# Attention weights of the first 16 head pairs: who divides by the sums, and how the small constant is added

## The chip, the cores and the metric

The kernel runs on one core of one Trainium2 chip. The metric is device time of one execution in microseconds (us), median of several runs. The engines are named as the profile names them: PE is TensorE's matmul, PEld its weight load, DVE is VectorE, ACT is ScalarE, POOL is GpSimd, SP is SyncE, which here issues DMAs. Line numbers such as L387 are lines of the kernel before.

## The reference

Three stages follow one another: attention in a window of 128 tokens with a bias that falls with distance, then an expert layer with a maximum of three products, then one with a gate.

```
scores = scale * q @ k.T ;  scores = where(mask, scores + bias, -1e9)      # 4 batches, 8 heads, 576 tokens, 64 wide
attn = exp(scores - max) ;  attn = attn / (sum(attn) + 1e-09) ;  x = attn @ v
h = max(max(x @ w1, x @ w2), x @ w3) ;  x = h @ w_out                      # 512 -> 768 -> 512, 2304 tokens
out = (silu(x @ w_gate) * (x @ w_val)) @ w_out2                            # 512 -> 1536 -> 512
```

## The kernel before

Attention is cut into units. A unit is 128 queries (or the last 64 of a batch) of one pair of heads; there are 80 units. The pairs are gone through in the order of `ORDER`, four pairs of heads for each entry. The first four entries of `ORDER` are called `NATIVE`; they are 16 pairs of heads and 24 units (8 + 4 + 8 + 4). Their scores are plain fp32 products, where the other 56 units use products of fp32r halves.

Each unit passes through four pieces, and pieces of following units are emitted between one another:

- `st_scores`: PE forms the scores of both heads; DVE picks the window (L358), adds the bias and takes the row minimum of the negated scores (L363); ACT takes the exponential and its row sums `sm`, one number for each of 128 rows and 2 heads (L368).
- `st_normalise`: 1e-9 is added to the 128x2 tile `sm` (on POOL at L376 for the native units, on DVE at L380 for the others), DVE takes the reciprocal `rc` (L382), and each head's 128x128 tile `z` is multiplied by its column of `rc`. Which engine does that is given by two letters, one for each head: `NORM0` for the first `K0` pairs (L385), `NORM` = "aa" (ACT for both, L391) for the others. "p" is POOL (L387), "v" is DVE (L389), "a" is ACT (L391).
- `st_transpose`: PE transposes both heads (L400), ACT copies the result out of PSUM (L412, or L408), and POOL masks it into two triangles (L416).
- `st_values`: PE multiplies by the values (L430 for native units), ACT rounds the result into the tile `x` (L436, L441), and POOL (or for the very first pairs DVE) forms the rest that rounding left (L107, the helper `low`).

The first expert layer is cut into six chunks of 384 tokens. A chunk's up products (18 groups of 12 matmuls, L156 to L158, all on the tile `x`) can begin when all four pairs of its tokens are through attention. The weights are prepared on the way: a raw pair of words goes through ACT (L118), three operations of DVE (L121, L122, L124), ACT again (L129) and DVE (L107). `spread` lays attention pieces, weight preparations and groups of matmuls between one another:

```
a0[0]()
spread(a0[1:], conv[:C0])                          # 12 native units, 2 weight tiles
spread(u[0], conv[C0:], a1[:cut1], early=EC)       # chunk 0, 7 weight tiles, 12 native units
spread(u[1][:SPLIT], conv_o, a1[cut1:] + a2[:cut2])
```

With the numbers set here `cut1` is all of `a1`, so all 24 native units lie in the first two of these stages. From this order and from planned durations and priorities a planner then fixes one instruction order for each engine, and each engine runs its own in that order: an instruction that waits holds up all that stands behind it on its engine. The chunks, the second layer and its token and weight preparation follow in the same manner; the second layer runs from about 460 us on.

Of the kernel before, what the change touches and what calls it, by code (L numbers as in the profile page):

```python
# [8 lines left out]
F32 = mybir.dt.float32  # L9
# [4 lines left out]
ALU = mybir.AluOpType  # L14
# [6 lines left out]
P = 128  # L21
# [36 lines left out]
N1, N2 = 21, 25  # L58
MB, TB, VB = 3, 1, 2
WARM, WN = 24, 256  # L60
NORM0, K0 = "pv", 16
AH = 0, 100
EC = 0
SPLIT = 12
# [7 lines left out]
def kernel(ctx: ExitStack, tc, *args):  # L72
    n = len(NATIVE)
    qs, ks, qks = (dict(zip(u, x)) for u, x in ((NATIVE, args), (NATIVE, args[n:]), (ORDER[n:], args[2 * n:])))
    vv, w123, wo1, wgv, wo2, out = args[-6:]
# [10 lines left out]
    nc = tc.nc  # L86
# [99 lines left out]
    def up_groups(c):  # L186

        n = CT
        m = {}

        def group(f, e):
            xt = x_t[c]
            ps = ps_m.tile([P, 512], F32, tag="m", name="ps1")
            for k in range(KD):
                mm3(ps[:, :n], w1[f, e], k * P, xt[k][:, 0, :n], xt[k][:, 1, :n], k == 0, k == KD - 1)
            with tc.high_priority(HIGH):
                if e == 0:
                    m[f] = tmp.tile([P, CT], F32, tag="m0", name="m0")
                    nc.scalar.copy(m[f][:, :n], ps[:, :n])
                else:  # L200
                    nc.vector.tensor_tensor(out=m[f][:, :n], in0=ps[:, :n], in1=m[f][:, :n], op=ALU.max)
                if e == 2:
                    ht = hp.tile([P, 2, n], F32R, tag="h", name="h")
                    pool_round(ht[:, 0, :], m[f][:, :n])
                    low(nc.gpsimd, ht[:, 1, :], m[f][:, :n], ht[:, 0, :])
                    hs[c, f] = ht

        return [lambda f=f, e=e: group(f, e) for f in range(NF1) for e in range(3)]
# [32 lines left out]
    small = ea("small", 2)  # L241
# [4 lines left out]
    bias = att.tile([P, H, P], BF16, name="bias")  # L246
    later = att.tile([P, 2, P], mybir.dt.int16, name="later")
    edge = att.tile([P, H, P], BF16, name="edge")


    first = {}
# [52 lines left out]
    def native(b, s):  # L304


        return (b, s) in NATIVE
# [64 lines left out]

    def st_normalise(u):
        m = u.mq
        if native(u.b, u.s):
            nc.gpsimd.tensor_scalar(  # L376
                out=u.sm[:m], in0=u.sm[:m], scalar1=1e-9, scalar2=1.0, op0=ALU.add, op1=ALU.mult
            )
        else:
            nc.vector.tensor_scalar(out=u.sm[:m], in0=u.sm[:m], scalar1=1e-9, scalar2=None, op0=ALU.add)  # L380
        rc = small.tile([P, 2], F32, tag="rc", name="rc")
        nc.vector.reciprocal(out=rc[:m], in_=u.sm[:m])  # L382
        for a in range(2):
            za, ra = u.z[:m, a], rc[:m, a:a + 1]
            how = (NORM0 if todo.index((u.b, u.s, u.p)) < K0 else NORM)[a]  # L385
            if how == "p":
                nc.gpsimd.tensor_scalar(out=za, in0=za, scalar1=ra, scalar2=1.0, op0=ALU.mult, op1=ALU.mult)  # L387
            elif how == "v":
                nc.vector.tensor_scalar(out=za, in0=za, scalar1=ra, scalar2=None, op0=ALU.mult)  # L389
            else:  # L390
                nc.scalar.activation(out=za, in_=za, func=AF.Copy, scale=ra)  # L391
# [125 lines left out]
    for t in range(len(units) + LV):  # L517
        if t >= LV:
            u = units[t - LV]
            steps.append(lambda u=u: soon(st_values, u))  # L520
            if t + 1 == len(units) + LV or (units[t + 1 - LV].b, units[t + 1 - LV].s) != (u.b, u.s):
                done_at.append(len(steps))
        if 0 <= t - LT < len(units):
            steps.append(lambda u=units[t - LT]: soon(st_transpose, u))
        if 0 <= t - LN < len(units):
            steps.append(lambda u=units[t - LN]: soon(st_normalise, u))
        if t < len(units):
            u = units[t]
            if u.j == SUBS[u.s][0]:
                i = todo.index((u.b, u.s, u.p))  # L530
                if i == 0:
                    steps.append(begin)
                steps.append(lambda u=u, i=i: (soon(st_scores, u), prep_next(i + 1), load_next(i + 2)))
            else:
                steps.append(lambda u=u: soon(st_scores, u))
# [246 lines left out]
        nc.tensor.matmul(ps[:, :WN], cold[:, :P], cold[:, :WN], start=True, stop=True)  # L782

    make_identity(nc, ident)
    tab, ones = zp.tile([P, 2, P], F32, tag="z", name="tab"), zp.tile([P, 2, P], F32, tag="z", name="ones")
    nc.gpsimd.iota(tab, pattern=[[0, 2], [1, P]], base=0, channel_multiplier=-1, allow_small_or_imprecise_dtypes=True)
    nc.vector.tensor_scalar(out=later, in0=tab, scalar1=0.0, scalar2=None, op0=ALU.is_gt)
# [16 lines left out]
    u = [up_groups(c) for c in SEQ]  # L804
# [142 lines left out]
```

## Time and profile before

| what | value |
|---|---|
| median of 3 runs | 856.21 us (856.02 to 856.42) |
| the profiled execution, its own time | 856.89 us |
| its span, first to last instruction | 855.2 us |
| PE busy | 836.0 us, 98% |
| DVE, ACT, POOL busy | 612.2, 422.9, 391.1 us |
| granted clock, mean | 0.996 of full speed |

Busy times are sums over one profiled execution. About 1.7 us of its time lie outside the span. A busy PE is not PE at its peak, since the ends of pipelined matmuls are modelled; the weight loads, one for each matmul, show better how densely it works.

### The profile page before, as it was taken

Reading aid. Unit: us, or ns where it says so; the run is one execution under the profiler, and the core shown is the slowest. Engines: PE = TensorE matmul, PEld = TensorE weight load, DVE = VectorE, ACT = ScalarE, POOL = GpSimd, SP = SyncE. Lnnn points to the kernel's source line nnn. Section 1 sums busy time; section 2 is a strip of 40 time slices with the busy share of each in tenths; the row PEclk is TensorE's granted clock in tenths of the full one; section 3 lists DMA queues with packets and bytes.
Section 4 is the critical chain, followed back from the end, with each engine's and each line's share of the span. In section 5 each row is a group of like instructions: output and inputs, shape, how many; then the busy total and the mean of one; then the engine's idle time right before and its main releaser. Section 6 shows DMA issues by size and latency. Waiting matters only on the chain.

```text
span 855.2 us, 14694 instructions
## 1 busy us (share of the span) xinstructions
PE 836.0 (98%) x4760; PEld 783.1 (92%) x4760; DVE 612.2 (72%) x1568; ACT 422.9 (49%) x1146; POOL 391.1 (46%) x575
## 2 busy tenths in 40 slices
PE   8898998999999999999999999999999999999998
PEld 6687897999999999999999999999999999999996
DVE  7999799778777787638978989995564854443342
ACT  6775676777667667525445555543422422212220
POOL 3688888469877667744323232221421211211110
PEclk9999999999999999999999999999999999999999
DMA  9664334333322232303367397733938422837322
GB/s 324 213 216 132 106 120 136 102 119 103 99 87 87 81 115 82 108 20 117 116 236 256 118 377 272 273 112 124 366 122 282 140 74 74 285 110 247 110 74 98
DMA packets 62780, 133.34 MB, mean 156 GB/s; under 512 B 6768, under 2 KB 24176, under 8 KB 61552
## 3 DMA queue, kind: packets, MB, share of 16 engines
q1 hardware_dynamic: 59248, 127.69, 44.2%
q10 hardware_dynamic: 3456, 4.72, 1.5%
q8 instruction: 37, 0.61, 0.3%
q14 instruction: 39, 0.32, 0.1%
HBM read 96.99 MB, written 35.39 MB: 155 GB/s over the span
## 4 chain that ended last, share of the span: by engine, by line
PE 79%; DVE 7%; POOL 5%; ACT 3%; issue 3%; DMA 2%; ACTq 0%; SPq 0%; POOLq 0%; DVEq 0%
PE ps L157 8%; PE ps L156 8%; PE ps L158 8%; PE pg L684 7%; PE pg L683 7%; PE pg L685 7%; PE po L765 6%; PE po L764 6%; PE po L763 6%; PE pc L684 3%; PE pc L683 3%; PE pc L685 3%; PE pv L447 2%; PE pt L400 1%; DVE wr L124 1%
## 5 line engine op out<-in xcount | busy, mean ns | idle before, releaser
L107 POOL TENSOR_TENSOR act<-h,act 128x384 fp32r<-128x384 f32 x72 | 79.9, 1130 | 287.3 <-ACT act L129 258.1
L157 PE MATMUL ps<-x,w 128*128 128x384 f32 x432 | 147.8, 342 | 0.7 <-POOL x L107 0.7
L158 PE MATMUL ps<-x,w 128*128 128x384 f32 x432 | 147.1, 341 | 0.0
L156 PE MATMUL ps<-x,w 128*128 128x384 f32 x432 | 146.4, 344 | 0.0
L683 PE MATMUL pg<-ya,u 128*128 128x384 f32 x360 | 120.6, 335 | 1.2 <-ACT s L706 1.2
L684 PE MATMUL pg<-ya,u 128*128 128x384 f32 x360 | 121.1, 336 | 0.0
L685 PE MATMUL pg<-ya,u 128*128 128x384 f32 x360 | 120.5, 335 | 0.0
L764 PE MATMUL po<-u,act 128*128 128x512 f32 x216 | 85.2, 395 | 0.0
L765 PE MATMUL po<-u,act 128*128 128x512 f32 x216 | 85.1, 396 | 0.0
L763 PE MATMUL po<-u,act 128*128 128x512 f32 x216 | 83.9, 389 | 0.0
L157 PEld LDWEIGHTS ps<-x,w 128*128 128x128 f32 x432 | 81.8, 189 | 1.9 <-POOL x L107 0.9
L416 POOL TENSOR_SCALAR_AFFINE_SELECT t<-pk 128x512 fp32r<-128x512 f32 (+2 forms) x128 | 74.0, 600 | 19.9 <-DVE pk L107 17.0
L156 PEld LDWEIGHTS ps<-x,w 128*128 128x128 f32 x432 | 81.4, 190 | 1.6 <-issue 1.0
L692 DVE TENSOR_TENSOR u<-pg,s 128x384 f32<-128x384 f32 x72 | 39.7, 553 | 59.8 <-PE pg L685 59.6
L158 PEld LDWEIGHTS ps<-x,w 128*128 128x128 f32 x432 | 81.7, 189 | 0.2 <-issue 0.2
L683 PEld LDWEIGHTS pg<-ya,u 128*128 128x128 f32 x360 | 67.6, 188 | 5.3 <-ACT s L706 1.5
L684 PEld LDWEIGHTS pg<-ya,u 128*128 128x128 f32 x360 | 67.6, 188 | 4.6
L368 ACT ACTIVATE z<-z,mn 128x128 f32<-128x128 f32 (+1 forms) x160 | 63.2, 398 | 10.8 <-DVE mn L363 9.6
L685 PEld LDWEIGHTS pg<-ya,u 128*128 128x128 f32 x360 | 67.6, 188 | 0.5
L720 ACT ACTIVATE h<-s 128x384 f32<-128x384 f32 x36 | 18.9, 524 | 91.1 <-DVE s L692 91.1
L118 ACT ACTIVATE wf<-wr 128x512 f32<-128x512 f32 (+2 forms) x57 | 40.0, 701 | 29.3 <-DVE wr L124 14.7
L692 DVE TENSOR_TENSOR u<-pc,u 128x384 f32<-128x384 f32 x72 | 39.9, 554 | 17.9 <-PE pc L685 17.5
(122 smaller groups left out, 2085.7 us busy)
## 6 DMA issues: line engine op xcount, KB each, us to landing
ya<-a_dram SPq DMA_DIRECT2D x56, 384.0 KB, 4.7
a_dram<-ya SPq DMA_DIRECT2D x42, 384.0 KB, 5.2
wr<-wgv SPq DMA_DIRECT2D x24, 512.0 KB, 4.6
wr<-w SPq DMA_DIRECT2D x9, 1024.0 KB, 5.2
qkr<-qk SPq DMA_DIRECT2D x32, 288.0 KB, 2.8
o_dram<-acc SPq DMA_DIRECT2D x36, 256.0 KB, 2.8
acc<-o_dram SPq DMA_DIRECT2D x36, 256.0 KB, 2.7
wr<-wo SPq DMA_DIRECT2D x12, 512.0 KB, 4.4
```

Source lines behind the costliest of these rows:

```text
L107: eng.tensor_tensor(out=out, in0=raw, in1=head.bitcast(F32), op=ALU.subtract)
L156: nc.tensor.matmul(ps, wh, xt_h, start=first, stop=False)
L157: nc.tensor.matmul(ps, wh, xt_l, start=False, stop=False)
L158: nc.tensor.matmul(ps, wl, xt_h, start=False, stop=last)
L416: nc.gpsimd.affine_select(out=t[:, i, :n, :, :m], in_=w[:, :n, :, :m], compare_op=op, fill=0.0, base=0, pattern=[[0, n], [0, 2], [-sign, m ...
L683: nc.tensor.matmul(o, wh, y[:, 0], start=first and k == 0, stop=False, skip_group_check=True)
L684: nc.tensor.matmul(o, wh, y[:, 1], start=False, stop=False, skip_group_check=True)
L685: nc.tensor.matmul(o, wl, y[:, 0], start=False, stop=k == 1, skip_group_check=True)
L692: nc.vector.tensor_tensor(out=o, in0=x, in1=y, op=ALU.add)
L763: nc.tensor.matmul(po, ah, w[:, 0], start=j == 0, stop=False)
L764: nc.tensor.matmul(po, ah, w[:, 1], start=False, stop=False)
L765: nc.tensor.matmul(po, al, w[:, 0], start=False, stop=j == PASS - 1)
```

## The change

`NORM0` goes from "pv" to "va": in the 24 native units the first head's tile is multiplied on DVE and the second on ACT, where it was POOL and DVE. And for all 80 units 1e-9 is added on DVE, as the sum of two tensors, with a new tile `eps` of 128x2 that one memset fills at the start; before, it was POOL's sum with a constant for the native units and DVE's sum with a constant for the others.

```diff
-NORM0, K0 = "pv", 16
+NORM0, K0 = "va", 16
...
+    eps = small.tile([P, 2], F32, tag="eps", name="eps", bufs=1)
...
     def st_normalise(u):
         m = u.mq
-        if native(u.b, u.s):
-            nc.gpsimd.tensor_scalar(
-                out=u.sm[:m], in0=u.sm[:m], scalar1=1e-9, scalar2=1.0, op0=ALU.add, op1=ALU.mult
-            )
-        else:
-            nc.vector.tensor_scalar(out=u.sm[:m], in0=u.sm[:m], scalar1=1e-9, scalar2=None, op0=ALU.add)
+        nc.vector.tensor_tensor(out=u.sm[:m], in0=u.sm[:m], in1=eps[:m], op=ALU.add)
         rc = small.tile([P, 2], F32, tag="rc", name="rc")
...
     make_identity(nc, ident)
+    nc.vector.memset(eps, 1e-9)
```

## Rows read from the trace of the kernel before

**Rows 1.** Stages: length, busy us (x) of PE, PEld, DVE, ACT, POOL; clock; DMA.

```profile
0.00:35.00 35.00, 28.92 (x172) 20.59 (x172) 29.56 (x126) 22.73 (x80) 18.00 (x43) 0.95 0.85 299
35.00:88.00 53.00, 48.68 (x299) 42.55 (x300) 46.58 (x112) 35.40 (x102) 43.45 (x63) 0.99 0.48 160
88.00:130.00 42.00, 40.99 (x253) 37.58 (x252) 37.44 (x115) 29.51 (x100) 35.34 (x53) 0.97 0.37 116
130.00:200.00 70.00, 67.11 (x421) 65.00 (x420) 58.28 (x200) 50.26 (x156) 47.11 (x87) 1.00 0.39 120
200.00:365.00 165.00, 165.00 (x1041) 161.37 (x1040) 120.75 (x439) 110.03 (x352) 121.88 (x217) 1.00 0.30 94
```

**Rows 2.** Chain that ended last, between 0 and 88 us: shares by line.

```profile
by line: issue 17.3%; POOL t L416 8.8%; POOL z L387 6.8%; ACT z L368 6.1%; PE sc L349 5.8%; DVE wr L124 5.5%; ACT wf L118 4.4%; POOL x L107 4.1%; ACT w L129 4.1%; POOL sm L376 3.8%; POOL r L107 3.5%; DMA qz<-q 3.2%; DVE sc L358 2.8%; DVE z 
```

**Rows 3.** Instruction groups, 0 to 88 us: xcount | busy us, mean ns | idle before, releaser.

```profile
L387 POOL TENSOR_SCALAR z<-z,rc 128x128 f32<-128x128 f32 x24 | 18.4, 765 | 7.5 <-DVE rc L382 6.0 <-PE sc L349 0.4 <-ACT x L436 0.4
L376 POOL TENSOR_SCALAR sm<-sm 128x2 f32<-128x2 f32 x24 | 6.8, 282 | 13.3 <-ACT z L368 10.5 <-ACT x L436 1.4
L389 DVE TENSOR_SCALAR z<-z,rc 128x128 f32<-128x128 f32 x24 | 8.0, 335 | 0.1
L382 DVE RECIPROCAL rc<-sm 128x2 f32<-128x2 f32 x24 | 3.8, 160 | 3.3 <-POOL sm L376 2.9
L121 DVE TENSOR_SCALAR wf<-wf 128x1024 int32<-128x1024 int32 x9 | 7.7, 859 | 0.2 <-ACT wf L118 0.2
L107 DVE TENSOR_TENSOR kl<-qkr,r 128x384 fp32r<-128x384 f32 x4 | 3.4, 862 | 0.0
```

**Rows 4.** Lines by themselves over the whole span: duration ns min/median/max.

```profile
L387 POOL TENSOR_SCALAR z<-z,rc x24: 366/424/1607, 9.6 to 82.9; 128x128 f32<-128x128 f32 x24
L376 POOL TENSOR_SCALAR sm<-sm x24: 191/192/1034, 6.7 to 80.1; 128x2 f32<-128x2 f32 x24
L389 DVE TENSOR_SCALAR z<-z,rc x24: 268/307/505, 9.5 to 80.9; 128x128 f32<-128x128 f32 x24
L391 ACT ACTIVATE z<-z,rc x112: 385/398/422, 97.3 to 361.4; 128x128 f32<-128x128 f32 x80, 64x128 f32<-64x128 f32 x32
L380 DVE TENSOR_SCALAR sm<-sm x56: 150/324/979, 95.9 to 360.2; 128x2 f32<-128x2 f32 x40, 64x2 f32<-64x2 f32 x16
L121 DVE TENSOR_SCALAR wf<-wf x57: 267/428/1498, 15.1 to 683.7; 128x512 int32<-128x512 int32 x36, 128x256 int32<-128x256 int32 x12, 128x1024 int32<-128x1024 int32 x9
L107 DVE TENSOR_TENSOR kl<-qkr,r x64: 406/562/1362, 67.7 to 336.2; 128x384 fp32r<-128x384 f32 x32, 128x256 fp32r<-128x256 f32 x32
L107 DVE TENSOR_TENSOR pk<-pt,pk x48: 275/409/426, 104.7 to 377.6; 128x256 f32<-128x256 f32 x32, 128x128 f32<-128x128 f32 x16
```

**Rows 5.** L380 alone by stretch: DVE busy (x), granted clock, DMA share.

```profile
88.00:200.00 112.00, 9.57 (x22) 0.99 0.38 119
```

**Rows 6.** Who waited for whom, 0 to 88 us: us in total, times, longest.

```profile
PEld pv L430 <- POOL t L416: 6.2, 8, 1.7
DVE rc L382 <- POOL sm L376: 2.9, 5, 1.0
```

**Rows 7.** Instructions of PE's weight loads in order of time, 83.7 to 90.5 us (x: how many merged).

```profile
83.74 0.19 PEld L158 LDWEIGHTS ps<-x,w 128*128 128x128 f32 x1
85.01 0.19 PEld L430 LDWEIGHTS pv<-t,rv 128*64 128x64 f32 x2 [1.08 <-POOL t L416]
86.35 0.42 PEld L430 LDWEIGHTS pv<-t,rv 128*64 128x64 f32 x6 [1.15 <-POOL t L416]
...
87.43 0.33 PEld L158 LDWEIGHTS ps<-x,w 128*128 128x128 f32 x1
...
89.99 0.33 PEld L157 LDWEIGHTS ps<-x,w 128*128 128x128 f32 x1
90.31 0.19 PEld L158 LDWEIGHTS ps<-x,w 128*128 128x128 f32 x1
```

**Rows 8.** The stage around them, columns as in rows 1.

```profile
80.00:90.00 10.00, 8.27 (x44) 7.39 (x42) 7.29 (x10) 4.39 (x11) 9.56 (x12) 0.84 0.18 58
```

## The prediction

> **What bounds the kernel now.** I read the busy times by stage first [rows 1]. From 200 to 365 us PE is busy in all of the time, and its weight loads in 161.4 of 165 us: there nothing but PE's own work sets the time. In the first 88 us this is not so. The loads are busy 20.6 of 35 us and 42.6 of 53 us, so against the dense stage (0.978 busy) about 13.6 + 9.3 = 23 us of loading time are missing; from 88 to 200 us it is 3.5 + 3.5 = 7 us more. What PE does later has to be done anyway, so a microsecond won or lost in the first 88 us, where all 24 native units lie, should arrive at the end nearly whole. That is where the change acts.
>
> The second view is the chain that ended last in these 88 us [rows 2]. It jumps from engine to engine: POOL's masks, POOL's multiplications (L387, 6.8% of 88 us = 6.0 us), POOL's sums (L376, 3.8% = 3.3 us), ACT's exponentials, DVE's weight preparation. So no engine alone bounds this stretch; it is the latency of the attention pieces, laid through queues that are nearly full. How full, is in rows 1: DVE 76.1 of 88 us, POOL 61.5, ACT 58.1. DVE is the fullest, and that is the danger for a change that gives it more to do.
>
> The third view is the spread of durations [rows 4]. POOL's multiplication takes 0.366 us at best, 0.765 us in the mean [rows 3] and 1.607 us at worst, and POOL's sum over two columns ranges from 0.191 to 1.034 us. ACT's same multiplication stays within 0.385 to 0.422 us. DVE's instructions of one tensor and a constant (L380, L121) stretch too, and so does a DVE sum of two tensors that both lie in SBUF (`kl`, up to 1.362 us), while one that reads PSUM (`pk`) stays at 0.275 to 0.426. DVE and POOL hold each other up; ACT is held up by neither.
>
> **Part 1: POOL's 48 instructions go.** POOL loses 18.4 + 6.8 = 25.2 us [rows 3] of its 61.5, or 41%. On the chain the two lines are 6.0 + 3.3 = 9.3 us. They are not all gained, since their successors stand in the same places. At their mean durations they are 6.0 / 0.765 = 8 multiplications and 3.3 / 0.282 = 12 sums. So −9.3 us, before what takes their place.
>
> **Part 2: ACT multiplies the second head.** 24 instructions of the shape of L391, 0.398 us each, 9.6 us more on an ACT that is busy 58.1 of 88 us: 77% after it. DVE keeps one head as before (24 of L389 at 0.335 us, now the first), so the later of the two heads is ACT's. Eight steps of the chain at 0.398 us: +3.2 us. Behind the waiting ACT instruction stand exponentials and PSUM copies of other units; that is a cost only where ACT waits for `rc`, and I leave it to the rivals.
>
> **Part 3: DVE adds 1e-9 as a sum of two tensors, for the native units.** No row shows two tensors of two columns. From below: DVE's reciprocal of the same size, 0.160 us, and the best L380, 0.150. From above: L380 between 88 and 200 us, 9.57 / 22 = 0.435 us, where POOL is busy 82.5 of 112 us, 74% [rows 1, 5]. After the change POOL would be busy about 36.3 of 88 us, 41%, so of the excess of 0.285 us I take 41/74: 0.150 + 0.158 = 0.31 us. Twelve on the chain: +3.7 us. The other twelve lie in DVE's queue and cost it 3.7 us as well. Against this, DVE is stretched less when 41% of POOL's work is gone: L389 is 24 x (0.335 − 0.268) = 1.6 us over its best, and the weight preparation and `kl` together some 5 us over theirs by the same reckoning (L121 alone 9 x (0.859 − 0.68) = 1.6, where 0.68 is my estimate from its smaller shape and the best L389; `kl` 4 x (0.862 − 0.55) = 1.25, estimated the same way). 41% of 6.6 us is 2.7 us. Net +1.0 us for DVE's queue.
>
> The Trainium skill, page "SBUF — State Buffer", section "Who interferes with whom", says that a DVE instruction with two SBUF inputs contends with a GpSimd instruction that reads SBUF, just as one in a two-port mode does. By that the sum of two tensors is no escape from POOL's lock; the `kl` rows above agree. Were it an escape, all 24 would cost 0.16 us and the sum would be 3.6 us better; the rows don't support that.
>
> **Part 4: the same sum in the other 56 units.** DVE did it before and does it after. From 88 to 200 us it is 22 x 0.285 = 6.3 us over its best [rows 5], from which the new form may recover nothing (it stretches like `kl`) or much. PE has only 1.0 + 2.9 us idle there [rows 1], so the gain is 0 to 3.9 us. I take −0.5 us: the `kl` instructions stretch nearly as far. From 200 us on PE covers all of it; if that cover went, 34 sums would count, at most 0.25 us each.
>
> **Part 5: PE's stalls and its clock.** PE's loads waited 6.2 us for POOL's masks L416 [rows 6]. The last two waits, 1.08 and 1.15 us, are followed by loads of 0.33 us instead of 0.19 [rows 7], until 90.3 us: the granted clock of 80 to 90 us is 0.84 [rows 8], so after waiting PE ran some 3.3 us at the lower of its two levels (1.2 instead of 2.4 GHz), which cost about half of that, 1.7 us. The POOL time ahead of these masks gets shorter; the masks themselves (8.8% of the chain) stay and are the next to be late. The wait is in the chain already, the clock isn't: I take half, −0.8 us.
>
> The memset of `eps` is one small DVE instruction before the first scores arrive; cost nothing, and 0.3 us (as long as a whole small tile) if DVE were late there. No DMA and no queue of SP changes.
>
> **Sum.** −9.3 + 3.2 + 3.7 + 1.0 − 0.5 − 0.8 = −2.7 us. The profiled execution took 856.9 us, so 854.2 us on its scale; it is 0.7 us above the median of the runs, 856.2, from which I predict 853.5 us.
>
> **Rivals.**
>
> *DVE becomes the bound (slower).* DVE is the fullest engine already. If the chain, with POOL out of it, simply runs through DVE's queue, nothing of the 9.3 us is gained and the 24 sums are paid in full: 24 x 0.31 = 7.4 us, less 2.7 us of relief, is +4.7 us: 861. With a best-case sum of 0.16 us it would be +1.1. It decides from the point where DVE's idle time of 5.4 us in the first 35 us and 6.4 us in the next 53 [rows 1] can't take the sums, since that idle time lies where DVE waits for PE. For it speaks that DVE, busy with weight preparation, must now also wait for ACT's exponential in its own order where POOL waited before (10.5 us of POOL's idle time were that, rows 3), with instructions of 1.2 us queued behind. Against it: DVE waited already, for POOL's sum, 2.9 us in these 88 us [rows 6].
>
> *It cancels (no change).* ACT's queue holds the second head back, or another POOL line (masks, rests of `x` and queries, 16% of the chain together) is late instead: the step gets shorter and the next wait longer. −1 to +1 us, 855.2 to 857.2.
>
> *POOL was the brake (much faster).* If POOL's shorter queue also brings the masks and `x` forward, so that most of the 6.2 us of PE's waits and the 1.7 us of clock go: −9.3 + 3.2 + 12 x 0.16 − 0.8 − 1.7 − 2 = −8.7 us, 847.5. For it: POOL is busy 43.5 of 53 us between 35 and 88 us, and PE's longest waits there are for it.
>
> Over all of these lies the planner: new durations and engines can give all queues another order, which could add or take 1 to 2 us anywhere in these 88 us; no row prices that.
>
> **How the numbers follow.** A difference of 0.2%, 1.7 us, is about what a measurement of this kernel can tell from no change. I give the forecast (−1.7 to −5) 0.43, much faster (beyond −5) 0.12, the cancelling 0.18 and DVE as the bound 0.27. So faster 0.55, same 0.18, slower 0.27. The range that leaves out about 2 in 10 runs from 848.5 (−7.7, about three quarters of the way from −5 to −8.7) to 860 us (+3.8 of the slow rival's +4.7). The forecast's own range is 851.2 to 854.5.
>
> **What would show it.** Right: L387 and L376 gone from POOL, which is busy about 25 us less (some 366); the sums of the native units at 0.2 to 0.35 us; the chain in the first 88 us without POOL's multiplications; the point where PE becomes dense (now about 92 us, after the slow clock) 2 to 4 us earlier, and the rest of the span only shifted. Wrong, on the slow side: DVE idle under 4 us in the first 35 us and PE waiting for DVE's `z`, or ACT's multiplication with long waits for `rc`. Wrong in the other part: sums of the other units at 0.16 us throughout, which would say that two tensors do escape POOL, or PE's loads between 200 and 365 us no longer dense, which would say that a reordering, not the edit, set the time.

## The result, and the profile of the changed kernel

The changed kernel takes 861.5 us (median of 6 runs, 858.68 to 863.36), the kernel before 856.13 beside it (6 runs, 855.93 to 856.42). The ratio is 1.0062, 95% interval 1.0045 to 1.0079: slower by 5.3 us, where I predicted 2.7 us faster. The profiled execution took 861.06 us with a span of 859.3.

First the stages of the changed kernel, columns as in [rows 1], the last three lines for stretches that matter below:

```profile
0.00:35.00 35.00, 28.12 (x161) 19.53 (x162) 30.81 (x143) 24.94 (x87) 7.10 (x19) 0.95 0.86 302
35.00:88.00 53.00, 52.06 (x305) 44.17 (x304) 46.49 (x121) 38.63 (x115) 29.86 (x38) 0.94 0.48 158
88.00:130.00 42.00, 40.27 (x257) 36.86 (x257) 37.31 (x114) 29.98 (x97) 37.30 (x54) 1.00 0.37 115
200.00:365.00 165.00, 165.00 (x1042) 161.32 (x1041) 121.97 (x441) 108.82 (x350) 120.14 (x216) 1.00 0.31 93
80.00:90.00 10.00, 9.45 (x58) 8.22 (x59) 9.41 (x13) 5.58 (x11) 8.97 (x11) 1.00 0.39 114
28.00:42.00 14.00, 11.73 (x44) 8.24 (x44) 9.70 (x39) 10.39 (x32) 5.24 (x8) 0.63 0.38 126
365.00:460.00 95.00, 91.37 (x527) 89.74 (x526) 70.15 (x131) 38.32 (x77) 26.29 (x33) 1.00 0.39 132
```

POOL lost 24.5 of its 61.5 us in the first 88, as planned, and the stretch from 80 to 90 us runs at full clock (it had 0.84, [rows 8]) with 8.22 us of loads instead of 7.39. The stage from 200 to 365 us is as dense as it was. Against that stand two stretches that the prediction did not single out, 28 to 42 us and 365 to 460 us. The same two in the kernel before:

```profile
28.00:42.00 14.00, 13.13 (x81) 10.19 (x81) 12.11 (x41) 10.42 (x35) 8.72 (x18) 0.88 0.46 152
365.00:460.00 95.00, 93.82 (x544) 92.66 (x544) 72.29 (x137) 39.93 (x82) 36.04 (x38) 1.00 0.37 128
```

PE's loads lose 1.95 us between 28 and 42 us at a clock of 0.63 instead of 0.88, and 2.9 us between 365 and 460 us, behind the last of the edited instructions (the last sum starts at 356 us).

The edited instructions themselves, in the groups of the first 88 us of the changed kernel (columns as in [rows 3]), and the sums over the whole span as in [rows 4]:

```profile
L387 ACT ACTIVATE z<-z,rc 128x128 f32<-128x128 f32 x24 | 9.6, 401 | 2.1 <-DVE rc L378 2.0
L385 DVE TENSOR_SCALAR z<-z,rc 128x128 f32<-128x128 f32 x24 | 8.9, 371 | 0.1
L376 DVE TENSOR_TENSOR sm<-sm,eps 128x2 f32<-128x2 f32 x24 | 4.8, 202 | 1.0 <-ACT z L369 1.0
...
L376 DVE TENSOR_TENSOR sm<-sm,eps x80: 143/279/943, 8.0 to 356.2; 128x2 f32<-128x2 f32 x64, 64x2 f32<-64x2 f32 x16
```

ACT's multiplication costs 0.401 us (I took 0.398) and DVE's native sum 0.202 (I took 0.31): the prices were right or too high. So the time must have gone elsewhere, and the waits are the first place to look. PE's loads in order of time, changed kernel:

```profile
26.69 0.52 PEld L350 LDWEIGHTS sc<-qkn 128*128 128x128 f32 x4 [1.03 <-DVE mn L364]
...
28.70 0.73 PEld L350 LDWEIGHTS sc<-qkn 128*128 128x128 f32 x4 [0.95 <-DVE mn L364]
...
31.59 0.93 PEld L350 LDWEIGHTS sc<-qkn 128*128 128x128 f32 x4 [1.78 <-DVE mn L364]
...
39.92 0.34 PEld L157 LDWEIGHTS ps<-x,w 128*128 128x128 f32 x1
...
41.56 0.19 PEld L158 LDWEIGHTS ps<-x,w 128*128 128x128 f32 x1
...
455.85 0.19 PEld L681 LDWEIGHTS pg<-ya,u 128*128 128x128 f32 x1
458.19 0.19 PEld L679 LDWEIGHTS pg<-ya,u 128*128 128x128 f32 x1 [2.16 <-ACT s L702]
```

Early, three groups of score loads wait for DVE's row minimum, and behind them PE works at half clock until 41.5 us (0.34 instead of 0.19 us a load, the 1.2 GHz level). Late, at 458 us, the second layer waits 2.16 us for ACT's copy `s`. Why that copy is late stands in ACT's timeline of the changed kernel:

```profile
453.86 0.53 ACT L716 ACTIVATE h<-s 128x384 f32<-128x384 f32 x1 [1.79 <-DVE s L688]
457.11 0.66 ACT L118 ACTIVATE wf<-wr 128x512 f32<-128x512 f32 x1 [2.73 <-DMA wr<-wo]
457.68 0.47 ACT L702 COPY s<-pg 128x384 f32<-128x384 f32 x1
```

The new plan has put `s` behind a weight conversion that waits 2.73 us for its DMA. In the kernel before, the copy ran ahead of the conversion that waited:

```profile
453.03 0.48 ACT L706 COPY s<-pg 128x384 f32<-128x384 f32 x1
...
458.15 0.67 ACT L118 ACTIVATE wf<-wr 128x512 f32<-128x512 f32 x1 [1.42 <-DMA wr<-wo]
```

A gap measures this place: from the last down product of the first layer to the first of the second it is 19.7 us before (438.7 to 458.4) and 22.0 us after (440.5 to 462.5), with the same number of products (103) in it. From there on both kernels take the same 378.6 us to the last gate product.

The copy `s` isn't the only wait there. What PE's loads waited for from 428 to 462 us (us in total, times, longest), first the kernel before, then the changed one:

```profile
PEld pg L683 <- ACT s L706: 1.5, 1, 1.5
```

```profile
PEld pg L679 <- ACT s L702: 2.2, 1, 2.2
PEld pg L679 <- ACT h L731: 1.4, 1, 1.4
PEld ps L156 <- ACT y L227: 1.0, 1, 1.0
PEld pg L679 <- ACT y L227: 0.3, 1, 0.3
```

All are waits for ACT, 1.5 us in sum before and 4.9 after. PE's products counted in the traces say the same: at the 2550th of 4760 the changed kernel is 0.8 us behind (429.1 against 428.3 us), at the first down product of the second layer 4.1 us, at the 4000th 4.2. So 3.3 of the 4.2 us by which these two profiled executions differ there arise between 428 and 462 us.

### The profile page after: what moved, and what is told of

Read it like the earlier page. It is cut to its first block, busy times and chain, and to the rows that moved or that the text cites. A ratio compares the mean times of both kernels' runs of the same rounds, so it can differ in the third digit from the quotient of the medians.

```text
span 859.3 us, 14657 instructions
## 1 busy us (share of the span) xinstructions
PE 838.9 (98%) x4760; PEld 783.1 (91%) x4760; DVE 612.8 (71%) x1593; ACT 431.8 (50%) x1170; POOL 362.1 (42%) x527
## 5 line engine op out<-in xcount | busy, mean ns | idle before, releaser
L412 POOL TENSOR_SCALAR_AFFINE_SELECT t<-pk 128x512 fp32r<-128x512 f32 (+2 forms) x128 | 77.0, 624 | 52.8 <-ACT pk L408 32.5
L387 ACT ACTIVATE z<-z,rc 128x128 f32<-128x128 f32 (+1 forms) x136 | 48.5, 396 | 27.2 <-DVE rc L378 26.6
```

Of the source, the lines that this page charges most:

```text
L412: nc.gpsimd.affine_select(out=t[:, i, :n, :, :m], in_=w[:, :n, :, :m], compare_op=op, fill=0.0, base=0, pattern=[[0, n], [0, 2], [-sign, m ...
```

## The experiments

Each kernel was timed in five rounds beside the kernel before on the same chip. "Order" below is the sequence of instructions on every engine. The planner makes a new one for each program; to hold it, the planned sequence of another program was written in as edges that fix the order and wait for nothing. An instruction that the edit moves to another engine keeps its place in that sequence. The edges are these lines:

```diff
+        for engine, rows in by.items():
+            rows.sort(key=lambda x: x[0])
+            for (_, a), (_, b) in zip(rows, rows[1:]):
+                tc.add_manual_dep(
+                    b, a.name, mybir.DependencyInfo(mybir.DependencyClass.NoSync, mybir.DependencyReason.DATA),
+                    reason="order of the other kernel",
+                )
```

| kernel | instructions | order | median us | ratio [95%] |
|---|---|---|---|---|
| e1 | changed | before | 856.38 | 0.9999 [0.9991, 1.0008] |
| e2 | before | changed | 862.24 | 1.0071 [1.0050, 1.0093] |
| e3 | multiplications only | its own | 856.19 | 0.9999 [0.9985, 1.0013] |
| e4 | sums only | its own | 851.04 | 0.9942 [0.9924, 0.9961] |
| e5 | sums only | before | 854.29 | 0.9978 [0.9969, 0.9986] |
| e6 | before | e4 | 854.19 | 0.9977 [0.9964, 0.9990] |
| e7 | changed | e4 | 856.54 | 0.9998 [0.9986, 1.0009] |
| e8 | changed | changed to 456 us, then before | 859.71 | 1.0034 [1.0022, 1.0046] |
| e9 | changed | changed, one DVE instruction moved | 861.20 | 1.0050 [1.0037, 1.0063] |
| e10 | changed | changed, one ACT instruction moved | 859.89 | 1.0041 [1.0025, 1.0056] |
| e11 | changed | changed, both moved | 859.93 | 1.0047 [1.0030, 1.0065] |
| e12 | multiplications only | before | 856.13 | 0.9998 [0.9987, 1.0009] |
| e13 | changed | changed to 59 us, then before | 856.56 | 0.9998 [0.9989, 1.0008] |
| e14 | changed | changed to 130 us, then before | 857.37 | 1.0010 [0.9999, 1.0021] |
| e15 | changed | e8, one DVE instruction moved | 857.42 | 1.0007 [0.9997, 1.0016] |
| e16 | changed | changed | 861.70 | 1.0049 [1.0033, 1.0066] |
| e17 | changed | e8 again | 858.35 | 1.0021 [1.0010, 1.0031] |
| e18 | changed | e15 again | 859.61 | 1.0031 [1.0021, 1.0042] |

**Instructions or order: e1 and e2.** Each takes one half of the change.

> The changed kernel's instructions, held on every engine in the order that the planner gave the kernel before (a moved instruction takes the place, in the planner's overall sequence, of the one it replaces). Theory ORDER (the loss is the planner's new order: weight preparation ahead of scores near 30 us, and ACT's wait for a DMA ahead of a copy that PE needs at 450 us): without the new order the loss goes, 853 to 856.5 us, ratio 0.996 to 1.000. Theory DVE (the sums and the lost POOL help load DVE's full queue, whatever the order): still slow, 859 to 863 us, ratio 1.004 to 1.008.

> The other way round: the instructions of the kernel before, in the order that the planner gave the changed kernel. Theory ORDER: slow like the changed kernel, 859 to 863 us, ratio 1.004 to 1.008, or slower still, since POOL's multiplications come back. Theory DVE: close to the kernel before, 855.5 to 858 us, ratio 0.999 to 1.002.

The new instructions in the old order cost nothing, 0.9999; the old instructions in the new order cost 1.0071, as much as the whole change. The late gap goes with the order too: 20.4 us in e1, 22.1 in e2. What slowed the kernel is the plan and not the instructions. No run holds a kernel in exactly its own order, so that the edges themselves cost nothing is argued: e1 and e12 come out at the time of the kernel before, and e9, the changed kernel held in its own order but for one instruction, at 1.0050 where the free one had 1.0062 and 1.0049 (e16). In e2 all of the difference is late: its profile is 0.3 us ahead of the kernel before at the 2550th product and 4.0 us behind at the 4000th.

**The parts alone, planned freely: e3 and e4.**

```diff
-NORM0, K0 = "pv", 16
+NORM0, K0 = "va", 16
```

```diff
+        nc.vector.tensor_tensor(out=u.sm[:m], in0=u.sm[:m], in1=eps[:m], op=ALU.add)
```

The first is all of e3, the second (with `eps`, and for all 80 units) all of e4.

> Only the multiplications move (first head DVE, second ACT, 16 pairs); all sums stay where they were (POOL for the native units, DVE with a constant for the others); the planner is free. Theory ORDER: another order again, so the loss is drawn anew, 853 to 860 us, and where PE's stalls at 30 us and 450 us are absent the time is at or below 856. Theory DVE: the added sums are the load, so without them the kernel is faster than before, 852 to 855.5 us.

> Only the sums change (two tensors on DVE for all 80 units); the multiplications stay on POOL and DVE; the planner is free. Theory DVE: it carries the loss, 859 to 863 us. Theory ORDER: drawn anew, 854 to 861 us; the time follows whether PE waits at 30 us and at 450 us, not the DVE's busy time in the first 88 us (some 5 us more than before).

e3 is unchanged and e4 wins 0.58%, 851.04 us: it beats both kernels. Neither part slows the kernel by itself; each time the planner drew another order.

**The parts in fixed orders: e5, e6, e7 and e12.**

> The sums alone on DVE as two tensors (multiplications as before), held in the order of the kernel before on every engine. The sums alone with a free planner were 0.9942. Theory ORDER: that gain is the planner's order and not the sums, so in the old order it goes: ratio 0.998 to 1.001. Theory SUMS (24 sums fewer on POOL, and two tensors in place of a tensor and a constant, are worth 5 us themselves): 0.993 to 0.996.

> The instructions of the kernel before, in the order that the planner gave the kernel with only the sums changed. Theory ORDER: fast like that one, ratio 0.993 to 0.997. Theory SUMS: near the kernel before, 0.999 to 1.002.

> All of the changed kernel's instructions in the order of the kernel with only the sums changed: the change with a better order, a candidate to beat both kernels. Theory ORDER: 0.992 to 0.997, so the same instructions span 1.3% by order alone. Theory SUMS or DVE: the moved multiplications cost what the sums give, 0.997 to 1.003.

> Only the multiplications move (first head to DVE, second to ACT), the sums stay as before, and every engine keeps the order of the kernel before. Theory (at a fixed order the multiplications cost some 2 us and the sums win some 2 us, each by itself): 858.4 us, ratio 1.0022, as the quotient of the runs with both parts and with the sums alone in that order says. Rival (the cost comes only from both parts together, since DVE then has the sums and one head): ratio 0.9985 to 1.0010.

In the old order the sums are worth −0.22% (1.9 us), the multiplications nothing (e12), and both together nothing (e1). So I was wrong to expect of e12 that the multiplications cost 2 us by themselves: they take away what the sums win. e6 and e4 split the best kernel's gain: its order alone wins 0.23% with the old instructions, and its instructions the rest. In that order the multiplications take everything back (e7, 0.9998).

Where it goes can be followed in the traces, one execution each: PE's order is the same in e1, e5, e12 and the kernel before, so its nth weight load is the same instruction. Leads over the kernel before in us, with minus for behind:

| load (its time in the kernel before) | e1, both | e12, multiplications | e5, sums |
|---|---|---|---|
| 100th (20.4 us) | −1.5 | −2.1 | −0.7 |
| 450th (82.1 us) | −0.2 | −0.6 | 0.0 |
| 500th (93.6 us) | +3.6 | +3.2 | +2.0 |
| 800th (144.5 us) | +2.3 | +1.4 | +1.9 |
| last (850.9 us) | +1.4 | +1.1 | +1.9 |

All three win at the masks, between the 450th and the 500th load, where the low clock of the kernel before [rows 7] is gone too. From 80 to 90 us the loads of e1 are busy 8.66 us, where the kernel before had 7.39 (columns as in [rows 1]):

```profile
80.00:90.00 10.00, 10.00 (x66) 8.66 (x65) 9.20 (x13) 5.41 (x15) 8.22 (x10) 1.00 0.19 58
```

The kernels with the multiplications then lose 1.3 and 1.8 us again, at two places. In e1 they are:

```profile
107.50 0.19 PEld L158 LDWEIGHTS ps<-x,w 128*128 128x128 f32 x1 [0.47 <-ACT m L201]
...
120.68 0.20 PEld L406 LDWEIGHTS pt<-ident,z 128*128 128x128 f32 x2 [1.25 <-PE ps L159]
```

In e12 these waits are 1.00 and 1.27 us. In e5 and the kernel before the first is absent and the second is 0.82 and 0.67 us. In e1 another 0.8 us goes between 430 and 456 us. The timings give e1 and e12 less than these leads, since the profiled execution of the kernel before took 856.89 us, more than its median, and those of e1 and e12 less than theirs. Why ACT's copy `m` is late there, no run shows.

**Where in the order: e8, e13, e14 and e17.** The changed instructions keep their own order up to one of PE's products and follow the old one behind it:

```diff
+    matmuls = [n for n, k in enumerate(one) if type(by[k]).__name__ == "InstMatmult"]
+    cut = matmuls[UNTIL]
+    head = [k for k in one[:cut]]
+    done = set(head)
+    whole = head + [k for k in two if k not in done]
```

> The changed kernel in its own planned order up to the 2550th matmul (about 400 us), and from there in the order of the kernel before. If the loss has two places, near 30 us and near 450 us, the second one (2.3 us more between the last product of the first layer and the first down product of the second) goes and the first stays: ratio 1.002 to 1.0045. If all of the loss comes from the first 100 us it stays at 1.005 to 1.008; if all came from 450 us it goes to 0.999 to 1.001.

> The changed instructions, in their own order up to PE's 200th product (about 41 us) and in the order of the kernel before behind it. Theory (the early loss is made by PE's waits for DVE at 26 to 32 us and the lower clock that follows): the whole early loss is there, ratio 1.0025 to 1.004 as with the own order up to 400 us (1.0034). Rival (the loss is made between 41 and 400 us, in the rest of attention): ratio 0.999 to 1.001, as with the old order throughout.

> The same with the boundary at PE's 600th product (about 103 us), behind the last native unit. Theory: as e13, 1.0025 to 1.004, or less where the old order gains something between 41 and 103 us. Rival (41 to 103 us makes it): e13 at 1.000 and this at 1.003; if both are at 1.000, the loss lies between 103 and 400 us.

The boundaries lie later than these expectations say. They were set by a count of the program's products, and the trace has more product records than that. In the traces PE keeps the changed kernel's sequence for 292, 738 and 2696 products, until 59 us in e13, 130 us in e14 and 456 us in e8, and has that of the kernel before from there on.

Up to 59 us the new order costs nothing, up to 130 us 0.10% with an interval that reaches zero, up to 456 us 0.34% and, timed again as e17, 0.21%; the whole of it costs 0.62% and 0.49% (e16). So about half of the loss lies behind 456 us. The first 59 us, where the profile showed the waits for DVE and the low clock, carry none that stays once the old order follows.

e8 leaves the changed order just ahead of the late wait. ACT's timeline of e8 has the copy `s` in front of the conversion again:

```profile
455.37 0.48 ACT L712 COPY s<-pg 128x384 f32<-128x384 f32 x1
...
458.66 0.67 ACT L120 ACTIVATE wf<-wr 128x512 f32<-128x512 f32 x1
```

PE's wait of 2.16 us is gone, and the other waits of that stretch stay (428 to 462 us, as above):

```profile
PEld pg L689 <- ACT h L741: 1.7, 1, 1.7
PEld ps L158 <- ACT y L229: 1.0, 1, 1.0
PEld pg L689 <- ACT y L229: 0.3, 1, 0.3
```

From the 2550th product to the first down product of the second layer it takes 31.5 us in e8 and 31.8 in e17, against 30.1 in the kernel before and 33.4 in the changed one. So 1.4 and 1.7 us of what e8 and e17 still lose stand in these waits for ACT, and not in attention.

**Single instructions: e9, e10, e11 and e15.** e9 moves one DVE weight preparation behind the score pieces that PE waited for. It is the one of 1.23 us here, in DVE's timeline of the changed kernel:

```profile
28.36 0.28 DVE L364 CUSTOM_DVE_ANT_0 z<-sc,bias 128x128 f32<-128x128 f32 x1
...
29.36 1.23 DVE L107 TENSOR_TENSOR w<-wr,w 128x1024 fp32r<-128x1024 f32 x1
...
31.24 0.29 DVE L364 CUSTOM_DVE_ANT_0 z<-sc,edge 128x128 f32<-128x128 f32 x1
31.45 0.08 DVE L364 DVE_READ_ACCUMULATOR2_ANT mn<- 128x1 f32 x1
```

```diff
-    nc, _, _ = build(lambda k: at.get(k, ident + 0.5))
+    moved = {217: at[318] + 0.5, 4914: at[4950] - 0.5}
+    nc, _, _ = build(lambda k: moved.get(k, at.get(k, ident + 0.5)))
```

217 is that DVE instruction (e9, e15), 4914 is ACT's copy `s`, put ahead of the conversion 4950 that waits for the DMA (e10); e11 has both.

> The changed kernel in its own order, with one DVE instruction elsewhere: the weight preparation w (1.23 us at 29.36 us) goes behind the next pair of score pieces, so that the minimum mn, for which PE's loads wait 1.78 us at 31.6 us, can come about 1.2 us earlier. Theory (the early loss is made by these waits of PE for DVE and by the lower clock that follows them): 1.2 us from the wait, and up to half of the 9 us that the loads then take at 0.33 instead of 0.19 us, so 857.5 to 860.3 us, ratio to the kernel before 1.0015 to 1.0048. Rival (the early loss is spread over many small waits in the queues): within 0.5 us of the changed kernel, 861 to 862, ratio above 1.0055.

> The changed kernel in its own order, with one ACT instruction elsewhere: the second layer's copy s stands directly ahead of the weight instruction that waits 2.73 us for a DMA at 457.1 us, instead of behind it. Theory (the late loss is this copy behind that wait): 2.2 us less, 859.3 us, ratio 1.0035, and a gap between the two layers' down products of 19.7 to 20.2 us instead of 22.0. Rival (the weights come late, and some other instruction waits in place of the copy): gap above 21.3 us, ratio 1.0052 to 1.0065.

> Both moves at once. Theory: the two losses add up, so the two savings do; 855.5 to 858 us, ratio 0.999 to 1.002. Rival (early time won is given back at the later wait for the DMA, or the other way round): no better than the better of the two by more than 0.5 us.

> The own order up to about 400 us and the old one behind it, with the one DVE instruction of e9 moved. Theory (e9's early gain was given back at the late wait, which is gone here): below e8's 859.7 us by 1 to 2.5 us, ratio 1.0005 to 1.002. Rival (the move wins nothing, since the next queue waits instead): 1.003 to 1.004, as e8.

e10's gap falls to 20.7 us and e11's to 20.4, most of the way to 19.7, so the copy behind the DMA wait makes most of that gap. Its time falls less, to 1.0041, and its interval overlaps that of the changed kernel: three shorter waits of PE, 0.74, 0.51 and 0.24 us, stand where one of 2.16 us stood, and the second layer takes 379.8 us to the last gate product instead of 378.6. e9 won nothing that can be told apart, and e11 no more than e10. The profile of e9 shows what else the late wait can do, PE's loads in order of time:

```profile
457.43 0.19 PEld L689 LDWEIGHTS pg<-ya,u 128*128 128x128 f32 x1 [2.36 <-ACT s L712]
457.54 0.19 PEld L690 LDWEIGHTS pg<-ya,u 128*128 128x128 f32 x1
457.71 0.32 PEld L691 LDWEIGHTS pg<-ya,u 128*128 128x128 f32 x1
458.02 0.33 PEld L689 LDWEIGHTS pg<-ya,u 128*128 128x128 f32 x1
...
461.18 0.19 PEld L690 LDWEIGHTS pc<-ya,u 128*128 128x128 f32 x1
```

Here PE falls to its lower clock level for 3.5 us behind the wait, which makes the gap 23.8 us; e16's profile has the same stretch (gap 23.7), the first profile of the changed kernel and e2's have not (22.0 and 22.1). e15 came out at 1.0007, and I took that for a gain of 2.3 us by the moved instruction against e8, which had run on another chip. Both were then timed once more, on one chip:

> The kernel of e8 again, on one chip with that of e15. Theory (the loss belongs to the order: one DVE instruction of 1.2 us ahead of the scores, on any chip): ratio 1.0025 to 1.004, clock 0.994 in most runs. Rival (the low clock was that chip's): ratio 1.000 to 1.0015, clock 0.996 to 0.998 in most runs.

> The kernel of e15 again, on the same chip as e17. Theory: at least 1.3 us below e17, clock 0.996 to 0.998. Rival: within 0.7 us of e17.

e18 is 1.26 us slower than e17, not faster. The moved instruction has no gain that holds, and the theory that DVE's weight preparation makes the early loss falls with it.

**The clock: e16.**

> The changed kernel once more beside these. Theory (part of its loss is PE at its lower clock at about 30 to 41 us, in most runs but not all): ratio 1.005 to 1.0065, with runs from 858 to 863 us whose granted clock runs from 0.998 to 0.992, about 0.86 us for each 0.001. Rival (the clock follows the waits and costs nothing of its own): the times of its runs don't follow their clock.

Over its 12 runs (the first 6 and e16) the changed kernel goes from 858.7 and 859.0 us at a mean clock of 0.998 to 862.7 to 863.5 at 0.992, 0.65 us for each 0.001 by a straight line. The mean clock is 0.9942 there and 0.9967 in 124 runs of the kernel before, whose own line has 0.27 us for 0.001. By these two slopes the lower clock is 0.7 to 1.6 us of the 5 us; it is the companion of the waits, and not the whole of the loss, since e2 loses as much at 0.997.

## Why the prediction was wrong

**The step that failed is the remark on the planner.** The prediction said that "new durations and engines can give all queues another order, which could add or take 1 to 2 us anywhere in these 88 us; no row prices that". The order alone moved the time by +6.1 us (e2, interval 4.3 to 8.0) and, drawn again for e4, by −2.0 (e6). And it wasn't confined to the 88 us: by two timings each, some 2.4 us of the loss (0.62 − 0.34% and 0.49 − 0.21%) lie behind 456 us, where e8 and the changed kernel differ by an ACT copy that stands behind a wait for a DMA, and the profiles put another 1.4 to 1.7 us between 428 and 456 us, at other waits for ACT. Neither has to do with attention. The prediction's own sign of a reordering, loads no longer dense between 200 and 365 us, did not appear (161.32 of 165 us): it watched another stretch. A term of this size belonged in the range, which ended at 860, and on both sides.

**The sum itself was off too.** At a fixed order −2.7 us was predicted and −0.1 measured (e1, interval −0.8 to +0.7), the outcome of the rival that cancels. By parts:

- Parts 1 and 2 took −6.0 + 3.2 = −2.8 us for POOL's multiplications and ACT's in their place; e12 has −0.2 us (−1.1 to +0.8). ACT's duration was right. What failed is the reading of the chain: time taken out of POOL's steps came back as waiting. In e12's profile PE is 2.1 us behind at the 100th load, 3.2 us ahead behind the masks, and 1.8 us of that are gone by the 800th load. The sign that I had named, PE dense 2 to 4 us earlier, did appear (3.6 us in e1), but the rest of the span was not only shifted.
- The sums went better than the terms. From part 1's −3.3, part 3's +3.7 and +1.0 and part 4's −0.5 they should cost 0.9 us; e5 has −1.9 us (−2.7 to −1.2). The sums cost 0.236 us in e5 and not 0.31, which is 24 x 0.074 = 1.8 us of that difference of 2.8, if all 24 count. Scaling the price by POOL's busy share was wrong: POOL is busy 55.2 of 88 us in e5 and 37.2 in e1, and the sums cost 0.236 and 0.240 us. Of the "some 5 us" of relief in part 3 only 2.9 are worked out there; no row gives the rest.
- The parts don't add: −0.2 and −1.9 make −0.1 together. Both shorten POOL's queue ahead of the masks, and behind these the leads of 3.2 and 2.0 us make 3.6 together: most of it can be bought only once.
- Part 5 was right in its place: the waits for the masks fell from 6.2 us [rows 6] to 2.6, and the low clock at 80 to 90 us is gone. The clock fell elsewhere, at 31 to 41 us, in the profiled execution.

**The rivals.** DVE as the bound would have made 861 us. That this is close to the measured time is a coincidence: DVE has its 24 sums in e1 as well, without a loss. Its signs half appeared (DVE idle 4.2 of the first 35 us where the sign was under 4, ACT's multiplication waiting 2.0 us for `rc`), so a sign can come near for a wrong reason. POOL as the brake is refuted at this order by e1, where POOL has neither the multiplications nor the sums. Its sum had also counted the clock twice, as −0.8 and within −1.7.

**The sum of two tensors.** The whole line runs from 0.143 to 0.943 us where the old one ran from 0.150 to 0.979 [rows 4], so it is no escape from POOL, as the Trainium skill, page "SBUF — State Buffer", section "Who interferes with whom", says of DVE instructions with two SBUF inputs. From 88 to 200 us its 128x2 sums took 0.402 us in the mean, the old ones 0.413. Why the native ones are cheaper stays open: e5 and e1, above, show that POOL's busy share alone doesn't set it.

**What stays open.** Between 59 and 456 us the new order costs 0.2 to 0.3%. The profiles put 1.4 to 1.7 us of that at the waits for ACT behind 428 us, but no run takes these waits away; whether the rest belongs to one wait isn't shown. Why e4's order is the better one wasn't taken apart either; its late gap is 19.8 us, so it is free of the late place.

## What to carry to other kernels

Where a planner orders the queues, time an edit twice: with the plan it gets, and in the order of the kernel before; here the first said +0.62% and the second nothing. Redrawing the order alone was worth −0.2 to +0.7%, more than the edit, and part of it struck 100 us behind the last edited instruction, so search the whole span for changed waits before explaining a loss by the edited lines. Where an order is cut at a count, look up in the trace when the cut comes: here it came 18 to 56 us later than planned, and that put it just ahead of the late wait. Parts that shorten the same queue share one gain; try each alone before both, since here one of them by itself beat both kernels.

## What the runs showed of the hardware

The granted clock of a stretch isn't a property of the order. e8 and e17 are the same kernel, and PE's loads wait for DVE 1.0, 0.95 and 1.8 us in both; from 28 to 42 us, columns as in [rows 1], e8 shows

```profile
28.00:42.00 14.00, 11.72 (x46) 8.31 (x43) 9.69 (x39) 10.20 (x31) 5.25 (x8) 0.63 0.40 138
```

and e17

```profile
28.00:42.00 14.00, 10.30 (x69) 7.62 (x70) 12.80 (x48) 11.64 (x39) 5.89 (x10) 1.00 0.50 163
```

so that runs of one kernel spread over mean clocks from 0.993 to 1.000 (e17) and over up to 4.8 us (the changed kernel). Every low stretch that was looked at came behind waits of PE of about 1 us or more, but such waits aren't always followed by one: the wait of 2.16 us at 458 us was not, the one of 2.36 us in e9 was.
